# One GELU square moved a slot later, one weight split cut in two, in a fused attention and MLP kernel

## The chip, the core and the metric

The kernel runs on one core of a Trainium2 chip. The core has a matrix engine (TensorE, PE in the profile; its weight loads are PEld), a vector engine (VectorE, DVE), an engine for activation functions (ScalarE, ACT), a general engine (GpSimd, POOL) and a queue that issues transfers (SyncE, SP). Each engine works through its own queue of instructions, and they wait for one another by semaphores. The metric is the device time of one execution in microseconds (us); lower is better.

## The reference

One sequence of 2048 tokens of width 576 goes through softmax attention with 32 heads of width 18 and through an MLP with 4608 hidden units behind a layer norm; a gate mixes the two.

```python
x = A_x                                          # (1, 2048, 576)
g = sigmoid((x * gate_w).sum(-1, keepdims=True))
# a: attention, 32 heads of 18
qkv = x @ wqkv                                   # wqkv (576, 1728)
scores = einsum("bhqd,bhkd->bhqk", q, k) * 18 ** -0.5
a = (softmax(scores) @ v) @ wo                   # heads joined, wo (576, 576)
# b: MLP
h = gelu(layernorm(x) @ w1 + b1)                 # tanh form, w1 (576, 4608)
b = h @ w2 + b2                                  # w2 (4608, 576)
return g * a + (1 - g) * b
```

## The kernel before

Everything is float32. Where a product runs in the faster rounded form (float32r), an operand is split in a rounded high part and a low part, and three products are added: high by high, low by high, high by low. So every weight and activation has a copy that rounds it (on ACT) and a subtraction that leaves the rest (on DVE or POOL).

**Prologue (to 216 us).** The tokens come in four blocks of 512. For each block x is transposed, and Q, K (`qk_group`, nine groups of 128 columns) and V (`v_group`) are made and written to memory. The 1728 columns of `wqkv` come in seven pieces. `load_w` fetches a piece by three transfers (four chunks of 128 rows; the last 64 rows twice), into a buffer of which there are two. `split_w` splits it: for each run of chunks one copy on ACT (line 752) and one subtraction (line 753) on DVE, or on POOL for the fourth to the sixth piece. Each piece holds five chunks of 288 columns, 1440 elements a partition, except the narrower first and fifth. The first two pieces are split in two runs, chunks 0 to 2 and chunks 3 and 4; the others in one run. The third piece (n = 2) holds columns 416 to 703; it is split on DVE just ahead of the second `qk_group`, and the fourth group, columns 384 to 511, is the first to use it. A group multiplies chunk by chunk: the high weights by both halves of x, then the low weights by the high half, so its third matmul is the first that needs the subtraction's result. The same engines make the statistics of the layer norm there, DVE most of all.

**The loop (216 to about 2150 us).** Attention runs over 32 units (a pair of heads and half of the queries), each with 16 key chunks, in 512 steps. Beside it runs the MLP, as a stream of pieces that `fill` puts between the steps. A step has two calls of `s2`: each makes two score matmuls (line 267, one for each head of the pair, on the two halves of the array's rows) and two exponentials (line 270). After each call there is a round of the pass ahead, `s1_round`: two score matmuls (line 227), whose row maxima DVE takes (line 229); these maxima are needed for a later unit. All score tiles come from `score_bank`, which goes through five PSUM banks in turn. After every second step `pv` multiplies the probabilities of two key chunks by V (line 285).

The order is written out by hand. `run_due` closes a slot: it counts the slot, issues what was deferred to it (`defer(n, f)`: n slots later), and then background work such as weight splits. A pass over two steps has eight slots, in this order: `s2`, piece 0 of the MLP and a round, slot end; piece 1, slot end; `s2`, piece 2 and a round, slot end; piece 3, slot end; `s2`, piece 4 and a round, slot end; piece 5, slot end; `s2`, piece 6 and a round, slot end; `pv`, what is left of the maxima's transposition (line 244, copied by ACT at line 246), slot end. After this, piece 0 comes again with its `s2`.

**The hidden layer.** `h_pair` makes two tiles of 128 hidden units by 512 tokens: 27 times two matmuls (line 484). There are 72 such pairs. At a pair's end DVE adds the bias to the second tile (line 504) and ACT to the first (Identity, line 505). Then comes the tanh form of GELU for both tiles, h = 1 ahead of h = 0: ACT squares z (line 537), POOL adds a constant and multiplies by z (`first`, two instructions), ACT takes Tanh (line 535, `second`), POOL adds 1, multiplies by z, and splits the result in `hh` and `hl` (`parts`, four instructions; all of POOL's at line 180). The squares are deferred by 2 slots, `first` by 3 slots for h = 1 and by 4 for h = 0; `second` comes when a count of POOL's work says that it is through, `parts` two slots later. Pairs end mostly in piece 6, so the squares are issued behind the next `pv`.

`out_pair` multiplies `hh` and `hl` by the second weights (48 matmuls, line 572) for a group of four tiles. In its middle the two row halves of PE exchange their banks; PE waits there for a semaphore that ACT raises (line 579) when it has seen the first half's end. The groups of the hidden layer and the output products alternate: after the first pair of a group come output products of the group before, after the second pair comes the next group's first pair. In the first quarter the MLP's weights are split as they are first used (line 392 on ACT, then POOL), and written to memory, from where the later quarters load them.

Of the kernel before, what the change touches and what calls it, by code (L numbers as in the profile page):

```python
# [10 lines left out]
AF = mybir.ActivationFunctionType  # L11
# [57 lines left out]
def gated_mix_kernel(ctx: ExitStack, tc: tile.TileContext, x, wqkv, wo, w1, b1, w2, b2, gate_w, out):  # L69
    nc = tc.nc  # L70
# [42 lines left out]
    def psum(pool):  # L113
        return pool.tile([P, TB], F32, name="ps")
# [28 lines left out]
    def defer(n, fn):  # L143
        later.append((slot[0] + n, fn))
# [7 lines left out]
    def queue_end(margin, fn):  # L152
        timed.append((pool_end[0] + margin, fn))
# [23 lines left out]
    def pool_op(n, fn, *args, **kw):  # L177

        pool_end[0] = max(pool_end[0], now[0]) + n * (1.36 if fn == nc.gpsimd.tensor_scalar else 2.7)
        fn(*args, **kw)  # L180
# [155 lines left out]
    def mlp():  # L336
# [3 lines left out]
        n = len(seq)  # L340
# [3 lines left out]
        def chunk(q):  # L344

            i, m = divmod(q, G // 2)
            return i, m, seq[i][1] * G + 2 * m
# [31 lines left out]
        def rounded(dst, src):  # L379
            pool_op(src.free_size(), nc.gpsimd.tensor_scalar, dst, src, 1.0, 1.0, op0=ALU.mult, op1=ALU.mult)  # L380
# [28 lines left out]
        def ready(table, key):  # L409
            while key not in table:  # L410
                bg.pop(0)[1]()
            return table[key]
# [46 lines left out]
        def h_pair(q, last, inner=False):  # L459

            i, m, fc = chunk(q)
            tb = seq[i][0]
            while q == 0 and q not in W1:
                cut[0] = 3
                yield 0
            wt = ready(W1, q)
            del W1[q]
            ps = [psum(ps_w) for _ in range(2)]
            if q == 0:
                slots = [(w_, 0, c) for c in range(9) for w_ in (0, 1)] + [(0, 1, c) for c in range(9)]  # L470
            else:
                slots = [(w_, s_, c) for c in range(9) for w_, s_ in ((0, 0), (1, 0), (0, 1))]
            change = tb + 1 < NB and (q + 1) % (npair // NB) == 0
            loaded = 0
            left = GAPS - piece[0]
            skip.clear()
            if (last and spent[0] >= behind[0]) or left < GAPS:
                left += GAPS
            ends = {k * 27 // left for k in range(1, left)}
            for k, (w_, s_, c) in enumerate(slots):  # L480
                for h in range(2):
                    r = slice(64 * h, 64 * h + 64)
                    y = low if q < NQ0 and s_ == 1 and c < 5 else Y[s_]
                    nc.tensor.matmul(ps[h], wt[w_][r, c, :], y[r, c, :], start=(k == 0), stop=(k == 26))  # L484
                if change and (k + 1 in ends or k == 26) and (k + 1) // 3 > loaded:

                    load_y(tb + 1, 0, loaded, (k + 1) // 3)
                    load_y(tb + 1, 1, loaded, (k + 1) // 3)
                    loaded = (k + 1) // 3
                if k == 26:  # L490
                    break
                if k + 1 in ends:
                    cut[0] = 1
                yield 231
                while k == 25 and open_pairs[0]:
                    cut[0] = 3
                    yield 0
            open_pairs[0] = 1
            if inner:

                extra = wp1.tile([P, 2, 9, P], F32R, name="w4").rearrange("p a b c -> p (a b c)")
            zs = [zp.tile([P, TB], F32, name="z") for _ in range(2)]
            b = [b1t[:, fc + h:fc + h + 1] for h in range(2)]
            nc.vector.tensor_scalar(zs[1], ps[1], b[1], None, op0=ALU.add)  # L504
            nc.scalar.activation(zs[0], ps[0], AF.Identity, bias=b[0])
            for h in (1, 0):
                z = zs[h]
                w = zp.tile([P, TB], F32, name="zz", bufs=3)
                if inner:
                    hh, hl = [extra[:, (2 * h + k) * TB:(2 * h + k + 1) * TB] for k in range(2)]  # L510
                else:
                    hh = hp.tile([P, TB], F32R, name="hh")
                    hl = hp.tile([P, TB], F32R, name="hl")


                def plus(c, w, z):

                    pool_op(TB, nc.gpsimd.tensor_scalar, w, w, c, 1.0, op0=ALU.add, op1=ALU.mult)
                    pool_op(TB, nc.gpsimd.tensor_tensor, w, w, z, op=ALU.mult)

                def parts(w=w, z=z, hh=hh, hl=hl, h=h, j=2 * m + h):
                    plus(1.0, w, z)
                    rounded(hh, w)
                    pool_op(TB, nc.gpsimd.tensor_tensor, hl, w, hh.bitcast(F32), op=ALU.subtract)
                    queue_end(-1000.0, lambda: HT.update({(i, j): (hh, hl)}))
                    if h == 0:
                        open_pairs[0] = 0

                def first(w=w, z=z, parts=parts):

                    plus(GC0, w, z)
                    queue_end(200.0, lambda: second(w, parts))

                def second(w, parts):
                    nc.scalar.activation(w, w, AF.Tanh, scale=GC1)
                    defer(2, parts)
                defer(2, lambda w=w, z=z: nc.scalar.activation(w, z, AF.Square))  # L537
                defer(4 - h, first)
            cut[0] = 2
            yield 231  # L540
# [61 lines left out]
        def load_y(tb, s_, c0=0, c1=9):  # L602
            inflow[0] = slot[0]
            if s_ not in Y:
                Y[s_] = big_tile()
            for h in range(2):
                dma_r(nc.sync, Y[s_][64 * h:64 * h + 64, c0:c1, :], y_scr[tb, s_, c0:c1].rearrange("c p n -> p c n"))
# [33 lines left out]
        def pair(q, ahead, last=False, inner=False):  # L641
            prep(q + ahead)
            yield from h_pair(q, last, inner)
            i, m, _ = chunk(q)
            if m == 1 and seq[i][1] == NG - 1:
                hidden[0] = seq[i][0]
                if i == n - 1:
                    defer(1, lambda: borrow_w2(q))
# [56 lines left out]
    with ExitStack() as a:  # L705
# [41 lines left out]
        def split_w(n, eng):  # L747
            c0 = W_CUT[n] if W_CUT[n] < 2 * D else W_CUT[n] - 2 * D
            hi, lo = [w_[:, :, c0:c0 + W_CUT[n + 1] - W_CUT[n]] for w_ in (W_QK if W_CUT[n] < 2 * D else W_V)]
            raw = wraw.pop(n)  # L750
            for cs in (slice(0, 3), slice(3, 5)) if n < 2 else (slice(0, 5),):
                nc.scalar.activation(hi[:, cs], raw[:, cs], AF.Copy)
                eng.tensor_tensor(lo[:, cs], raw[:, cs], hi[:, cs].bitcast(F32), op=ALU.subtract)  # L753

# [178 lines left out]
        for c in range(5):  # L933
            x_chunk(0, c)
            if c == 2:
                split_w(0, nc.vector)
                load_w(2)
        b1r = sm.tile([NFC, P], F32, name="b1r", bufs=1)
        for tb in range(NB):
            work = [(qk_group, (tb, mt)) for mt in (range(9) if tb < 2 else (4, 0, 1, 2, 3, 5, 6, 7, 8))] + [(v_group, (tb, t, n)) for t in range(4) for n in range(2)]  # L940
            for g, (fn, args) in enumerate(work):
                if tb == 0:
                    if g in W_AT:
                        n = W_AT[g]
                        split_w(n, nc.gpsimd if 2 < n < 6 else nc.vector)
                        if n + 2 < 7:
                            load_w(n + 2)
                    if g == 10:
                        nc.sync.dma_start(b2b, bcast_rows(b2, D))
                        nc.sync.dma_start(b1r, b1.rearrange("(c p) -> c p", p=P))  # L950
# [376 lines left out]
```

## Time and profile before

| what | us |
|---|---|
| median of 3 runs | 2234.97 (2234.52 to 2236.86) |
| the profiled execution's own time | 2236.32 |
| its span, first to last instruction | 2234.4 |

Busy time in us by stretch of the span:

| stretch | length | PE | PEld | DVE | ACT | POOL |
|---|---|---|---|---|---|---|
| 0 to 20 | 20 | 15.25 | 12.33 | 7.54 | 9.47 | 10.78 |
| 20 to 60 | 40 | 38.81 | 34.50 | 30.87 | 17.04 | 14.99 |
| 60 to 216 | 156 | 155.90 | 126.83 | 108.40 | 51.33 | 42.87 |
| 216 to 690 (weights split) | 474 | 469.44 | 325.79 | 355.09 | 342.11 | 291.99 |
| 690 to 2150 | 1460 | 1457.20 | 1017.91 | 1108.40 | 977.32 | 642.56 |
| 2150 to end | 84.4 | 77.56 | 63.55 | 34.92 | 29.84 | 0.00 |

A line of the timeline gives the start in us, the time to the end of the merged instructions, the engine, the line of the kernel, the operation, the tile written and those read, the shapes, how many instructions were merged, and in brackets the engine's idle time before them with what ended it. A line of the waits gives who waited for whom: us in total, how often, the longest. In the groups by line, the numbers behind the bar are busy time, mean ns of one, and idle time before them.

### The profile page before, as it was taken

How to read it: one execution, taken by the hardware profiler on the slowest of the kernel's cores; microseconds unless marked ns; L12 is line 12 of the kernel's file. 1: busy time of each engine (PE TensorE's matmuls, PEld its weight loads, DVE VectorE, ACT ScalarE, POOL GpSimd, SP SyncE). 2: the span in 40 equal slices, each digit the busy share in tenths (PEclk: the TensorE clock that was granted, in tenths of full speed). 3: DMA queues.
4: the chain of work that ended last, by engine and by line, in shares of the span. 5: the costliest groups of instructions: out<-in, count | busy, mean ns of one | idle time of the engine just before them, and what ended most of it. 6: DMA issues, size and time to landing. Idle time of an engine off the chain costs nothing.

```text
span 2234.4 us, 51590 instructions
## 1 busy us (share of the span) xinstructions
PE 2214.2 (99%) x20528; PEld 1580.9 (71%) x20528; DVE 1645.2 (74%) x2888; ACT 1427.1 (64%) x2655; POOL 1003.2 (45%) x1001
## 2 busy tenths in 40 slices
PE   8999999999999999999999999999999999999998
PEld 7878667766667766666767767767666666776768
DVE  6675777777777777777777777777776777777734
ACT  4333677777766666666666666666666666666671
POOL 4322766666664444444445444444444444444700
PEclk9999999999999999999999999999999999999999
DMA  8867555444464533333364323232454333242264
GB/s 265 273 218 224 186 173 161 146 159 147 154 199 135 189 107 115 122 120 103 113 178 157 122 92 122 98 123 100 129 168 144 108 120 122 91 143 100 81 217 167
DMA packets 164136, 329.23 MB, mean 147 GB/s; under 512 B 56846, under 2 KB 84106, under 8 KB 153166
## 3 DMA queue, kind: packets, MB, share of 16 engines
q1 hardware_dynamic: 161798, 322.19, 44.4%
q8 instruction: 162, 2.65, 0.5%
q10 hardware_dynamic: 1968, 3.70, 0.5%
q14 instruction: 80, 0.66, 0.1%
q0 software_dynamic: 128, 0.03, 0.0%
HBM read 233.47 MB, written 96.17 MB: 148 GB/s over the span
## 4 chain that ended last, share of the span: by engine, by line
PE 92%; DVE 3%; DMA 2%; ACT 1%; issue 1%; POOL 1%; SPq 0%; ACTq 0%; DVEq 0%; POOLq 0%
PE ps L285 20%; PE ps L572 20%; PE ps L484 20%; PE ps L267 13%; PE ps L227 11%; PE ps L882 3%; PE ps L1212 2%; PE ps L903 2%; DVE m L229 1%; DMA x<-in_B_w_dram 1%; ACT zz L537 0%; POOL w L180 0%; PE ps L758 0%; DMA p<-in_A_wqkv_dram 0%; PE ps L885 0%
## 5 line engine op out<-in xcount | busy, mean ns | idle before, releaser
L229 DVE TENSOR_REDUCE m<-ps 128x1 f32<-128x512 f32 x2048 | 1312.2, 684 | 409.4 <-PE ps L227 384.8
L270 ACT ACTIVATE p<-ps 128x512 f32<-128x512 f32 x1368 | 741.0, 596 | 380.7 <-PE ps L267 376.0
L484 PE MATMUL ps<-big,w 64*128 64x512 f32 x3708 | 568.0, 393 | 1.0 <-DVE z L504 0.6
L180 POOL TENSOR_SCALAR zz<-zz 128x512 f32<-128x512 f32 x288 | 178.4, 620 | 748.8 <-ACT zz L537 734.0
L270 ACT ACTIVATE ring<-ps 128x512 f32<-128x512 f32 x680 | 369.0, 596 | 189.1 <-PE ps L267 187.0
L572 PE MATMUL ps<-w,hh 64*128 64x288 f32 x4352 | 483.9, 294 | 1.8 <-DVE x L589 0.9
L267 PE MATMUL ps<-qa,ka 56*128 56x512 f32 x2048 | 459.6, 422 | 2.9 <-ACT p L270 1.7
L572 PEld LDWEIGHTS ps<-w,hh 64*128 64x128 f32 x4352 | 423.8, 187 | 30.3 <-DVE x L589 3.2
L227 PE MATMUL ps<-ka,qa 54*128 54x512 f32 x2048 | 433.5, 398 | 0.6
L484 PEld LDWEIGHTS ps<-big,w 64*128 64x128 f32 x3708 | 368.2, 187 | 67.7 <-DVE z L504 1.1
L180 POOL TENSOR_TENSOR zz<-zz,z 128x512 f32<-128x512 f32 x288 | 371.9, 1291 | 24.0
L267 PEld LDWEIGHTS ps<-qa,ka 56*128 56x128 f32 x2048 | 213.2, 184 | 220.8 <-DVE m L229 181.0
L572 PE MATMUL ps<-w,hl 64*128 64x288 f32 x2176 | 348.3, 292 | 0.8 <-POOL hl L180 0.8
L285 PE MATMUL ps<-p,vt 128*32 128x512 f32 x2560 | 322.9, 599 | 0.0
L227 PEld LDWEIGHTS ps<-ka,qa 54*128 54x128 f32 x2048 | 218.8, 185 | 25.2 <-DVE m L229 4.5
L572 PEld LDWEIGHTS ps<-w,hl 64*128 64x128 f32 x2176 | 231.5, 185 | 1.2 <-POOL hl L180 1.1
L180 POOL TENSOR_TENSOR hl<-zz,hh 128x512 fp32r<-128x512 f32 x136 | 176.8, 1300 | 11.4
L180 POOL TENSOR_TENSOR w<-x,w 128x576 fp32r<-128x576 f32 (+1 forms) x54 | 98.8, 1845 | 168.0 <-ACT w L392 147.8
L285 PE MATMUL ps<-ring,vt 128*32 128x512 f32 x1280 | 168.7, 599 | 0.0
L285 PEld LDWEIGHTS ps<-p,vt 128*32 128x32 f32 x2560 | 67.2, 109 | 142.3 <-issue 136.1
L589 DVE SCALAR_TENSOR_TENSOR x<-ps,x 128x288 f32<-128x288 f32 x256 | 104.0, 448 | 8.6 <-PE ps L572 8.3
L882 PE MATMUL ps<-big,wqk 128*128 128x512 f32 x432 | 108.6, 400 | 0.8 <-DVE wqk L753 0.8
(124 smaller groups left out, 1491.1 us busy)
## 6 DMA issues: line engine op xcount, KB each, us to landing
w<-w_scr SPq DMA_DIRECT2D x54, 1152.0 KB
w<-w_scr SPq DMA_DIRECT2D x108, 576.0 KB
x<-in_B_w_dram SPq DMA_DIRECT2D x72, 288.0 KB
w_scr<-w SPq DMA_DIRECT2D x18, 1152.0 KB
w_scr<-w SPq DMA_DIRECT2D x36, 576.0 KB
qa<-qk_scr SPq DMA_DIRECT2D x192, 72.0 KB
ka<-qk_scr SPq DMA_DIRECT2D x84, 144.0 KB
qk_scr<-hh SPq DMA_DIRECT2D x36, 256.0 KB
```

The lines of the kernel that those rows point to most:

```text
L180: fn(*args, **kw)
L227: nc.tensor.matmul(ps, qa[r0:r0 + 54, t * P:(t + 1) * P], ka[r0:r0 + 54, kb * TB:(kb + 1) * TB], start=True, stop=True)
L229: nc.vector.tensor_reduce(M4[u][:, h, t, kb:kb + 1], ps, axis=AX.X, op=ALU.max)
L267: nc.tensor.matmul(ps[h], ka[r0:r0 + 56, kc * P:(kc + 1) * P], qa[r0:r0 + 56, qb * TB:(qb + 1) * TB], start=True, stop=True)
L270: nc.scalar.activation(RING[n % 3][:, qb, h], ps[h], AF.Exp, scale=SCALE)
L285: nc.tensor.matmul(OB[u][r:r + 32, :], v[:, k, 19 * h:19 * h + 32], RING[c % 3][:, qb, h, :], start=(k == 0), stop=(k == NT - 1))
L484: nc.tensor.matmul(ps[h], wt[w_][r, c, :], y[r, c, :], start=(k == 0), stop=(k == 26))
L572: mm = nc.tensor.matmul(ps[nn][:, :ND], h_[r, tok], w_[p_][r, cs[nn]], start=(k == 0), stop=(k == 6 * G - 1))
L589: nc.vector.scalar_tensor_tensor(dst, ps[nn][:, :ND], 0.5, b2b[:, cs[nn]] if g == 0 else dst, op0=ALU.mult, op1=ALU.add)
L882: nc.tensor.matmul(ps, w_[:, c, ms], big[:, s_, :], start=(k == 0), stop=False)
L903: nc.tensor.matmul(ps[:, :ND], big[:, s_, tok], w_[:, c, cs], start=(k == 0), stop=False)
L1212: nc.tensor.matmul(ps[:, :ND], OT[b][2][:, s_, tok], w_part(w_, c)[:, cs], start=(k == 0), stop=(k == 13))
```

## The change

The square of the second tile (h = 0) is deferred by three slots and no longer by two; that of the first tile (h = 1) stays at two. And the third weight piece is split in two runs of chunks like the first two pieces: two copies on ACT (864 and 576 elements a partition) and two subtractions on DVE, in place of one each (1440).

```diff
@@ h_pair
                 def second(w, parts):
                     nc.scalar.activation(w, w, AF.Tanh, scale=GC1)
                     defer(2, parts)
-                defer(2, lambda w=w, z=z: nc.scalar.activation(w, z, AF.Square))
+                defer(3 - h, lambda w=w, z=z: nc.scalar.activation(w, z, AF.Square))
                 defer(4 - h, first)
             cut[0] = 2
             yield 231
@@ split_w
             raw = wraw.pop(n)
-            for cs in (slice(0, 3), slice(3, 5)) if n < 2 else (slice(0, 5),):
+            for cs in (slice(0, 3), slice(3, 5)) if n < 3 else (slice(0, 5),):
                 nc.scalar.activation(hi[:, cs], raw[:, cs], AF.Copy)
                 eng.tensor_tensor(lo[:, cs], raw[:, cs], hi[:, cs].bitcast(F32), op=ALU.subtract)
```

## The prediction

> **What bounds the kernel now.** I read the page first, then the list of what PE waited for, then ACT and PE in order of time at the places where the moved square stands, and last the first 45 us.
>
> ```profile
> span 2234.4 us, 51590 instructions
> PE 2214.2 (99%) x20528; PEld 1580.9 (71%) x20528; DVE 1645.2 (74%) x2888; ACT 1427.1 (64%) x2655; POOL 1003.2 (45%) x1001
> PE 92%; DVE 3%; DMA 2%; ACT 1%; issue 1%; POOL 1%; SPq 0%; ACTq 0%; DVEq 0%; POOLq 0%
> ```
>
> PE is busy for 99% of the span and makes 92% of the chain that ended last. So ACT, at 64%, matters only where PE must wait for one of its results. PE's own waits are short:
>
> ```profile
> PE ps L267 <- ACT p L270: 1.7, 8, 0.3
> PE ps L572 <- POOL hl L180: 0.8, 1, 0.8
> PE ps L882 <- DVE wqk L753: 0.8, 1, 0.8
> ```
>
> In the loop these rows hold a few microseconds in all, for ACT's exponentials 1.7 us in 8 waits; in the prologue 0.8 us behind the very line that the second edit splits. These figures are too small, though, since a PE row counts as busy until a modelled end. The first place below shows it: a matmul slips by 0.57 us, and the idle column says 0.18.
>
> How ACT makes PE wait: scores go through five PSUM banks in turn, an exponential pair takes two and a maximum round takes two. The second score matmul of a pair therefore writes the bank that the first exponential of the pair before has to have read. That exponential's end is the deadline that counts.
>
> **Edit 1, the second square, where a transpose stands ahead.** At a pair's end ACT runs Identity (L505), both squares (L537), then two exponential pairs, then Tanh (L535). Now the second square goes behind the first exponential pair. Nothing is added: 72 squares change place in ACT's queue, no DMA is moved, and neither SP's queue nor any other is passed. In 8 of the 72 pair ends the copy of the row maxima (L246) stands ahead of the squares, for the first time at 460 us and for the last at 1813 us. One of them:
>
> ```profile
> 460.19 0.27 ACT L246 ACTIVATE mr<-ps 32x128 fp32r<-32x128 f32 x1 [1.52 <-PE ps L244]
> 1813.31 0.27 ACT L246 ACTIVATE mr<-ps 32x128 fp32r<-32x128 f32 x1 [1.05 <-PE ps L244]
> ...
> 1012.26 1.13 ACT L537 ACTIVATE zz<-z 128x512 f32<-128x512 f32 x2
> 1013.30 2.00 ACT L270 ACTIVATE p<-ps 128x512 f32<-128x512 f32 x4
> 1013.35 0.40 PE L267 MATMUL ps<-qa,ka 56*128 56x512 f32 x1
> 1013.92 0.49 PE L267 MATMUL ps<-qa,ka 56*128 56x512 f32 x1 [0.18 <-ACT p L270]
> 1015.12 0.57 PE L267 MATMUL ps<-qa,ka 56*128 56x512 f32 x2
> ```
>
> The squares take the exponentials' time: four of them run without a gap, 0.48 us apart and 0.57 long. The first ends at 13.30 + 0.57 = 13.87 (I leave off the 1000), and PE's second matmul, which should have come with its partner at 13.35, starts at 13.92: 0.05 us for the semaphore, 0.57 us lost. After the change the first exponential starts one square earlier, 0.52 us, at 12.78; the matmul needs 12.78 + 0.57 + 0.05 = 13.40, so only 0.05 is lost. The square then costs the second pair: it starts at 12.78 + 0.48 + 0.48 + 0.52 = 14.26, as now, while PE comes 0.52 earlier. The next pair's second matmul, at 15.29 now (15.12 + 0.57 less a length of 0.40), would come at 14.77 and has to wait until 14.26 + 0.57 + 0.05 = 14.88: 0.11 lost. Net gain 0.41 us. At 460 us a Tanh and a weight copy right behind give it all back. I count 7 x 0.35 = 2.5 us gained, 0.35 because the halves of PE run out of step there.
>
> The Trainium skill (Trainium Kernel Development and Optimization, section "Performance Expectations") says that matmul busy time is a bad measure of the distance to the roofline, because matmuls are pipelined. The trace agrees: the row shows 0.18 us idle where 0.57 were lost. By busy time alone edit 1 could win 1.7 us at most; by the starts it is more.
>
> **Edit 1 elsewhere.** Where no transpose stands ahead, ACT has time to spare before the first exponential pair, and none or little behind it:
>
> ```profile
> 1050.31 1.15 ACT L537 ACTIVATE zz<-z 128x512 f32<-128x512 f32 x2
> 1051.90 1.09 ACT L270 ACTIVATE p<-ps 128x512 f32<-128x512 f32 x2 [0.45 <-PE ps L267]
> 1053.07 1.09 ACT L270 ACTIVATE ring<-ps 128x512 f32<-128x512 f32 x2
> 1054.04 0.63 ACT L535 ACTIVATE zz<-zz 128x512 f32<-128x512 f32 x1
> 1054.56 1.09 ACT L270 ACTIVATE ring<-ps 128x512 f32<-128x512 f32 x2
> 1054.05 0.40 PE L267 MATMUL ps<-qa,ka 56*128 56x512 f32 x2
> 1055.44 0.41 PE L267 MATMUL ps<-qa,ka 56*128 56x512 f32 x2
> 1051.02 0.62 POOL L180 TENSOR_SCALAR zz<-zz 128x512 f32<-128x512 f32 x1 [25.89 <-ACT zz L537]
> 1051.72 1.29 POOL L180 TENSOR_TENSOR zz<-zz,z 128x512 f32<-128x512 f32 x1
> ```
>
> Here the square now runs in a hole (0.45 us idle behind it) and is put into a dense stretch. It starts 0.12 us before the pair's end (Tanh to its neighbours shows this overlap: 54.04 against 53.07 + 1.09), at 52.87, and holds ACT 0.52 us (two squares in 1.15, one 0.63). The second pair moves from 53.07 to 53.39, Tanh and the third pair by the same 0.32. First deadline: 53.39 + 0.60 + 0.05 = 54.04 against 54.05, just kept. Second: 54.88 + 0.60 + 0.05 = 55.53 against 55.46 (the second of the pair, 0.02 behind its partner): 0.07 us lost. ACT's next idle time ends it. I count 21 such places from 690 us on: 1.5 us lost.
>
> Where weights are still being split, a weight copy (L392) follows that Tanh, and PE is already late:
>
> ```profile
> 515.67 1.09 ACT L270 ACTIVATE p<-ps 128x512 f32<-128x512 f32 x2
> 516.64 0.63 ACT L535 ACTIVATE zz<-zz 128x512 f32<-128x512 f32 x1
> 517.17 0.68 ACT L392 ACTIVATE w<-x 128x576 fp32r<-128x576 f32 x1
> 517.74 1.08 ACT L270 ACTIVATE p<-ps 128x512 f32<-128x512 f32 x2
> 518.04 0.84 PE L267 MATMUL ps<-qa,ka 56*128 56x512 f32 x2
> ```
>
> PE's pair takes 0.84 us instead of 0.40, its second matmul at 517.74 + 0.59 + 0.05 = 518.38. Every 0.32 us more is lost in full. Four places (351, 513, 567, 621 us): 1.3 us.
>
> Where products with the second weight follow (30 places), the dense stretch has a gap:
>
> ```profile
> 1066.07 1.09 ACT L270 ACTIVATE ring<-ps 128x512 f32<-128x512 f32 x2 [0.22 <-PE ps L267]
> 1067.34 1.09 ACT L270 ACTIVATE p<-ps 128x512 f32<-128x512 f32 x2 [0.18 <-PE ps L267]
> 1068.17 0.41 PE L267 MATMUL ps<-qa,ka 56*128 56x512 f32 x2
> L579 ACTq EVENT_SEMAPHORE  x1: 17/17/17, 1068.1 to 1068.1; - x1
> ```
>
> The square runs from 67.04, the second pair from 67.56 instead of 67.34, its first end with the semaphore at 68.21 against 68.18: 0.03 us each, 0.9 in all. The few other places I set at -0.2 us together.
>
> POOL waits for these squares, but it starts with the first one, which doesn't move, and needs 0.70 + 1.29 us (51.02 to 53.01) before it asks for the second; that now ends at 53.50 instead of 51.46, so POOL's work on it starts about 0.5 us late. The cover is POOL's idle time, 25.89 us at this place; without it, 0.5 us at each pair, 36 us. What waits behind the square on ACT is counted above; its own inputs are old.
>
> Edit 1: -2.5 + 1.5 + 1.3 + 0.9 - 0.2 = +1.0 us. Its bounds: all eight gains in full and no loss, 8 x 0.57 = -4.6 us; and 0.32 us at all of the 64 other places, +20 us. I stay with the sum, since it goes place by place.
>
> **Edit 2, the third weight piece.** Five chunks of 288 columns go through one copy on ACT and one subtraction on DVE; PE's fourth group waits for the whole.
>
> ```profile
> 17.61 1.41 ACT L752 ACTIVATE wqk<-p 128x1440 fp32r<-128x1440 f32 x1 [4.00 <-DMA p<-in_A_wqkv_dram]
> 10.53 1.49 ACT L752 ACTIVATE wqk<-p 128x864 fp32r<-128x864 f32 x2
> 19.05 1.66 DVE L753 TENSOR_TENSOR wqk<-p,wqk 128x1440 fp32r<-128x1440 f32 x1 [4.72 <-ACT wqk L752]
> 11.48 1.73 DVE L753 TENSOR_TENSOR wqk<-p,wqk 128x864 fp32r<-128x864 f32 x2
> 19.34 0.63 PE L882 MATMUL ps<-big,wqk 128*128 128x512 f32 x2
> 20.76 2.59 PE L882 MATMUL ps<-big,wqk 128*128 128x512 f32 x10 [0.80 <-DVE wqk L753]
> PEld ps L903 <- DVE wv L753: 0.4, 1, 0.4
> ```
>
> The second piece has the same size and is already cut: its two copies take 1.49 us, its two subtractions 1.73. So the split costs 0.08 us on ACT and 0.07 on DVE. By elements the first part is 3/5: 0.9 us of copy from 17.61 to 18.51, then 1.04 us of subtraction to about 19.6, the rest to 18.54 + 1.73 = 20.27 instead of 20.71. PE's third matmul of that group wants it at 19.34 + 2 x 0.235 = 19.81 (0.63 for two, less a length of 0.40, is the spacing) and started at 20.76: 0.95 us gained there. DVE is dense behind it, so its work comes 0.44 us earlier, and PE next waits for DVE at the last weight piece (L903, 0.4 us). There only DVE's 0.44 is kept. The first part no longer needs the two last transfers and may start before 17.61. I take -0.5; the bounds are +0.1 (extra instructions, nothing kept) and -1.0.
>
> **Sum.** +1.0 - 0.5 = +0.5 us on the profiled execution's own 2236.32 us (span 2234.4 and 1.9 around it). That execution is 1.35 us above the median of 2234.97. Carried to the median: 2235.5 us, which is no change; 0.2% (4.5 us) is about what a measurement of this kernel can tell from none.
>
> **The rivals.** *The bank swap waits for ACT (slower).* In the middle of an output product PE waits for a semaphore that ACT raises (L579), queued behind the second exponential pair. At 1068.1 it comes 0.2 us after that pair's last exponential was taken (67.34 + 0.49 = 67.83) and before its end at 68.43, so nothing shows that it waits for the end. Were it to wait for the end, each of the 39 pair ends with products behind would lose about 0.3 us: +12 us, 2247. It decides once the pair is later than the slack to PE's next half. *ACT's order was what delayed PE (faster).* If the exponentials behind the square keep their deadlines by other slack, no loss stands against the gains: -4.6 - 1.0, 2229.4 on the median. For it: both deadlines are missed by under 0.1 us. Against it: PE at 518 us is late already. *The loss is everywhere as with the weight copies (slower):* 0.32 us at all 25 pair ends of the first kind, +8.0 - 2.5 + 0.9 - 0.7: 2240.7. Against it: only 4 have a weight copy.
>
> **How the numbers follow.** Forecast 0.66; the swap 0.10 and the loss everywhere 0.08, both slower; the faster one 0.16. These give faster 0.16, within 0.2% 0.66, slower 0.18. The range goes from the faster rival to beyond the smaller slow one and leaves the swap out: 2229 to 2243.
>
> **What would show it.** ACT reads Identity, square, two exponentials, square at the pair ends. Near 1012 us the pair of score matmuls starts together; near 1050 us the second exponential pair starts 0.3 us later after the first; near 518 us PE's pair grows from 0.84 to about 1.15 us. Near 20 us PE's 0.80 us is gone, and the 0.4 us at L903 has grown. PE's waits for L579 stay near none. It is wrong if the semaphore rows of L579 move to the exponentials' ends, or if POOL's late half reaches PE (waits for hl above 0.8 us).

## The result, and the profile after

The changed kernel takes 2244.85 us (median of 5 runs, 2244.2 to 2247.33) against 2235.09 before (5 runs, 2234.52 to 2236.86): 1.0043 times the time of before, 95% interval 1.0032 to 1.0054. It is slower by some 10 us; I had forecast no change, and 2229 to 2243 as the range. The profiled execution took 2245.5 us, with a span of 2243.6 against 2234.4, so 9.2 us are to be found.

The page of the changed kernel, span, busy times and the chain by engine:

```profile
span 2243.6 us, 51653 instructions
PE 2223.8 (99%) x20528; PEld 1597.8 (71%) x20528; DVE 1649.8 (74%) x2889; ACT 1416.6 (63%) x2656; POOL 1003.0 (45%) x1001
PE 90%; DVE 3%; DMA 2%; ACT 2%; issue 1%; POOL 1%; SPq 0%; ACTq 0%; POOLq 0%; DVEq 0%
```

PE is "busy" for 9.6 us more with the same 20528 matmuls. So the loss sits inside what the page counts as busy, and the busy share alone can't show it. What PE's matmuls (PE) and its weight loads (PEld) waited for, after:

```profile
PE ps L267 <- ACT p L270: 1.8, 6, 0.4
PEld ps L267 <- ACT p L270: 8.5, 28, 0.8
PEld ps L267 <- ACT ring L270: 5.6, 19, 1.0
PE ps L572 <- POOL hl L180: 0.6, 1, 0.6
```

The same list before, for the weight loads:

```profile
PEld ps L267 <- ACT p L270: 7.3, 17, 0.7
PEld ps L267 <- ACT ring L270: 3.2, 7, 1.0
```

The matmuls wait for ACT hardly more than before, but their weight loads do 47 times in place of 24. The product with V is a good ruler for a stretch, as it needs both halves of PE. Two successive ones stand around the pair end that the prediction read near 1050 us. Before:

```profile
1049.52 1.07 PE L285 MATMUL ps<-ring,vt 128*32 128x512 f32 x8
1056.49 1.07 PE L285 MATMUL ps<-p,vt 128*32 128x512 f32 x8
```

and after:

```profile
1051.99 1.07 PE L285 MATMUL ps<-ring,vt 128*32 128x512 f32 x8
1059.21 1.07 PE L285 MATMUL ps<-p,vt 128*32 128x512 f32 x8
```

6.97 us became 7.22: 0.25 us lost at this one pair end, where I had worked out 0.07. Measured in this way at all 72 pair ends (PE's start 8.5 us behind the squares less its start 0.5 us ahead of them, after against before):

| pair ends | count | lost, us | predicted, us |
|---|---|---|---|
| hidden pair follows, no transpose ahead | 30 | 6.1 (0.23 each at most places) | 1.5 + 1.3 |
| output products follow, no transpose ahead | 34 | 5.3 (0.17 each at most places) | 0.9 |
| transpose ahead of the squares | 8 | -2.0 | -2.5 |
| prologue, to the loop's start | | -0.4 | -0.5 |

(The prediction's other places, -0.2, fall into the first two rows.) The four add up to 9.0 of the 9.2 us. The rest of the loop loses another 0.6 us (eight places, shown by the experiment with a late POOL, lose 0.9 there), and the stretch behind 2150 us is 0.4 us shorter.

### The profile page after: what moved, and what is told of

Same layout as the page of the kernel before. It is cut to its first block, busy times and chain, and to the rows that moved or that the text cites. A ratio compares the mean times of both kernels' runs of the same rounds, so it can differ in the third digit from the quotient of the medians.

```text
span 2243.6 us, 51653 instructions
## 1 busy us (share of the span) xinstructions
PE 2223.8 (99%) x20528; PEld 1597.8 (71%) x20528; DVE 1649.8 (74%) x2889; ACT 1416.6 (63%) x2656; POOL 1003.0 (45%) x1001
## 4 chain that ended last, share of the span: by engine, by line
PE 90%; DVE 3%; DMA 2%; ACT 2%; issue 1%; POOL 1%; SPq 0%; ACTq 0%; POOLq 0%; DVEq 0%
PE ps L285 20%; PE ps L572 19%; PE ps L484 19%; PE ps L267 13%; PE ps L227 11%; PE ps L882 3%; PE ps L1212 2%; PE ps L903 1%; DVE m L229 1%; DMA p<-in_A_wqkv_dram 1%; ACT p L270 0%; POOL w L180 0%; POOL zz L180 0%; DMA x<-in_B_w_dram 0%; PE ps L758 0%
## 5 line engine op out<-in xcount | busy, mean ns | idle before, releaser
L484 PE MATMUL ps<-big,w 64*128 64x512 f32 x3708 | 579.5, 393 | 1.0 <-DVE z L504 0.6
L572 PE MATMUL ps<-w,hh 64*128 64x288 f32 x4352 | 501.1, 293 | 1.8 <-DVE x L589 0.9
L267 PE MATMUL ps<-qa,ka 56*128 56x512 f32 x2048 | 480.5, 427 | 3.4 <-ACT p L270 1.8
L572 PEld LDWEIGHTS ps<-w,hh 64*128 64x128 f32 x4352 | 442.1, 186 | 27.2 <-DVE x L589 3.2
L227 PE MATMUL ps<-ka,qa 54*128 54x512 f32 x2048 | 454.0, 398 | 0.6
L484 PEld LDWEIGHTS ps<-big,w 64*128 64x128 f32 x3708 | 381.5, 187 | 60.9 <-DVE z L504 1.1
L267 PEld LDWEIGHTS ps<-qa,ka 56*128 56x128 f32 x2048 | 232.8, 184 | 227.0 <-DVE m L229 181.0
L572 PE MATMUL ps<-w,hl 64*128 64x288 f32 x2176 | 368.8, 292 | 0.6 <-POOL hl L180 0.6
L572 PEld LDWEIGHTS ps<-w,hl 64*128 64x128 f32 x2176 | 253.1, 185 | 1.0 <-POOL hl L180 0.8
L227 PEld LDWEIGHTS ps<-ka,qa 54*128 54x128 f32 x2048 | 233.7, 185 | 22.9 <-DVE m L229 5.3
```

Of the source, the lines that this page charges most:

```text
L227: nc.tensor.matmul(ps, qa[r0:r0 + 54, t * P:(t + 1) * P], ka[r0:r0 + 54, kb * TB:(kb + 1) * TB], start=True, stop=True)
L267: nc.tensor.matmul(ps[h], ka[r0:r0 + 56, kc * P:(kc + 1) * P], qa[r0:r0 + 56, qb * TB:(qb + 1) * TB], start=True, stop=True)
L572: mm = nc.tensor.matmul(ps[nn][:, :ND], h_[r, tok], w_[p_][r, cs[nn]], start=(k == 0), stop=(k == 6 * G - 1))
```

## What the trace shows at one pair end

ACT near 1050 us of the old count, changed kernel:

```profile
1052.78 0.63 ACT L537 ACTIVATE zz<-z 128x512 f32<-128x512 f32 x1
1054.44 1.09 ACT L270 ACTIVATE p<-ps 128x512 f32<-128x512 f32 x2 [1.03 <-PE ps L267]
1055.41 0.63 ACT L537 ACTIVATE zz<-z 128x512 f32<-128x512 f32 x1
1055.93 1.09 ACT L270 ACTIVATE ring<-ps 128x512 f32<-128x512 f32 x2
1056.88 0.65 ACT L535 ACTIVATE zz<-zz 128x512 f32<-128x512 f32 x1
1057.40 1.11 ACT L270 ACTIVATE ring<-ps 128x512 f32<-128x512 f32 x2
```

The order is the predicted one. The hole ahead of the first exponential pair has grown from 0.45 to 1.03 us, and behind it there is none: the second pair starts 1.49 us behind the first in place of 1.17, 0.32 later, as predicted. PE and its weight loads there, after:

```profile
1053.85 0.50 PE L267 MATMUL ps<-qa,ka 56*128 56x512 f32 x2
1055.11 0.47 PE L267 MATMUL ps<-qa,ka 56*128 56x512 f32 x2
1056.30 0.46 PEld L267 LDWEIGHTS ps<-qa,ka 56*128 56x128 f32 x2
1056.53 0.56 PE L267 MATMUL ps<-qa,ka 56*128 56x512 f32 x2
1057.93 0.64 PE L267 MATMUL ps<-qa,ka 56*128 56x512 f32 x2
```

and the second of them before, for the matmuls at 1054.05 that the prediction shows:

```profile
1053.83 0.19 PEld L267 LDWEIGHTS ps<-qa,ka 56*128 56x128 f32 x2
```

Before, both weight loads of the pair start together at 53.83, 0.22 us ahead of the matmuls. After, the first starts at 56.30 and the second, 0.18 long, not before 56.30 + 0.46 - 0.18 = 56.58. That is the end of the first exponential, 55.93 + 0.60 = 56.53, and 0.05 for the semaphore. So it is the weight load that waits for the bank.

How late may it be? The pair before this one answers that, since one of its two weight loads is late in the kernel before as well:

```profile
1052.55 0.18 PEld L267 LDWEIGHTS ps<-qa,ka 56*128 56x128 f32 x1
1052.64 0.41 PE L267 MATMUL ps<-qa,ka 56*128 56x512 f32 x2
1052.64 0.21 PEld L484 LDWEIGHTS ps<-big,w 64*128 64x128 f32 x2
```

Its partner started at 52.41, so this load is 0.14 us behind, and 0.09 us ahead of the matmul. The next weight loads (L484) are 0.19 long; the first starts at 52.64 together with the matmul, the second at 52.64 + 0.21 - 0.19 = 52.66, 0.11 us behind the late load. So only 0.02 us is lost. The three pairs in question, after:

```profile
1055.09 0.18 PEld L267 LDWEIGHTS ps<-qa,ka 56*128 56x128 f32 x1
1055.12 0.27 PEld L484 LDWEIGHTS ps<-big,w 64*128 64x128 f32 x2
1056.58 0.18 PEld L267 LDWEIGHTS ps<-qa,ka 56*128 56x128 f32 x1
1056.58 0.29 PEld L484 LDWEIGHTS ps<-big,w 64*128 64x128 f32 x2
1058.07 0.18 PEld L267 LDWEIGHTS ps<-qa,ka 56*128 56x128 f32 x1 [0.19 <-ACT ring L270]
1058.18 0.19 PEld L484 LDWEIGHTS ps<-big,w 64*128 64x128 f32 x2
```

Each late load comes 0.05 us behind the end of an exponential and now hardly ahead of its own matmul (at 55.12, 56.59 and 58.08). The matmul's row still starts on time, and so hides the loss, but the next weight load of that half again follows 0.11 us behind the late one (at 55.20, 56.68 and 58.18). The half is set back by 0.07, 0.10 and 0.09 us at the three pairs, less the 0.02 of before: 0.24 us together, about one matmul, and the product with V, for which both halves must be through, turns it into lost time. The matmul pairs show the growing lag: they take 0.47, 0.56 and then 0.64 us in place of 0.41. So the deadline is not the start of the matmul but some 0.11 us ahead of it. Over the whole trace a pair's second weight load starts less than 0.1 us ahead of its matmul 314 times before and 407 times after, and in 402 of the 407 the next weight load follows it by 0.10 to 0.12 us.

## The experiments

**Each edit alone.** The first run has the change's first edit, the second its second, on the kernel before:

```diff
-                defer(2, lambda w=w, z=z: nc.scalar.activation(w, z, AF.Square))
+                defer(3 - h, lambda w=w, z=z: nc.scalar.activation(w, z, AF.Square))
```

> Edit 1 alone: the second square a slot later, the third weight piece in one run as before. Theory A (ACT's queue: the square stands in ACT's dense stretch, the exponentials behind it come too late for PE's weight loads): all of the loss and none of the prologue's gain of 0.4 us, so 2245.3 us against 2235.1 before. Theory B (POOL: its work on the second tile starts 0.5 us later and reaches PE late): also 2245.3. Theory C (the split weight piece costs the time further on): 2235, as before.

```diff
-            for cs in (slice(0, 3), slice(3, 5)) if n < 2 else (slice(0, 5),):
+            for cs in (slice(0, 3), slice(3, 5)) if n < 3 else (slice(0, 5),):
```

> Edit 2 alone: the third weight piece in two runs, both squares where they were. A and B: 0.4 us faster than before, 2234.7, with PE's 0.8 us wait for the third piece gone. C: 2245.

The square alone: 2247.23 against 2236.09 us, ratio 1.0047 (1.0032 to 1.0062); a second time 1.0046 (1.0032 to 1.0060). The split alone: 2235.82, ratio 0.9997 (0.9988 to 1.0007). Theory C is out, the square makes the whole loss. By the trace the split does what it was to do (PE in the fourth group, changed kernel; before, the row broke off behind two matmuls):

```profile
19.47 2.73 PE L882 MATMUL ps<-big,wqk 128*128 128x512 f32 x11
17.04 1.50 ACT L752 ACTIVATE wqk<-p 128x864 fp32r<-128x864 f32 x2 [3.31 <-DMA p<-in_A_wqkv_dram]
18.00 1.73 DVE L753 TENSOR_TENSOR wqk<-p,wqk 128x864 fp32r<-128x864 f32 x2 [3.54 <-ACT wqk L752]
```

PE runs through, and the copy starts at 17.04 in place of 17.61, as the first run no longer needs the two last transfers. The loop starts 0.4 us earlier in the changed kernel and 0.9 us earlier with the split alone; in the traces without the split it starts between 0.3 us earlier and 0.6 us later than before, so the size of the gain is not settled, and on the whole time it is less than a comparison can show.

**ACT or POOL?** The next two pull the two theories apart. One lets ACT do a second square at the new place, and POOL wait for nothing new:

```diff
                 defer(2, lambda w=w, z=z: nc.scalar.activation(w, z, AF.Square))
+                if h == 0:
+                    defer(3, lambda hh=hh, z=z: nc.scalar.activation(hh, z, AF.Square))
```

> Both squares as before, and a second copy of the h = 0 square, written into a tile that POOL overwrites later, at the slot to which the change moves the square. POOL waits for nothing new. A: the loss of 0.2 us at 64 pair ends stays, and at the 8 with a transpose ahead there is now a loss of 0.5 us in place of a gain: 13 + 4, 2252 us. B: 2235, since POOL starts as before.

The other makes POOL late and leaves ACT's order as it was:

```diff
-                def first(w=w, z=z, parts=parts):
+                def first(w=w, z=z, parts=parts, h=h, hh=hh):
 
+                    if h == 0:
+                        nc.gpsimd.tensor_scalar(hh, z, 1.0, 1.0, op0=ALU.mult, op1=ALU.mult)
                     plus(GC0, w, z)
```

> Both squares as before, and one more POOL instruction (a rounding copy of 512 elements, 0.7 us with its gap) ahead of POOL's work on the second tile, so that all its work from there is 0.7 us later, more than the 0.5 us of the change. A: 2235 within 1 us. B: at least the loss of the change, 2245 to 2249.

The extra square: 2247.74 us, ratio 1.0050 (1.0035 to 1.0065). The loss stays with POOL as before, so ACT's queue is the cause of most of it; it is smaller than expected, 0.11 us at a pair end with output products behind and 0.18 with a hidden pair, for 0.17 and 0.24 with the moved square, and 1.6 us over the 8 with a transpose ahead, where 4 were expected. POOL late: 2240.89 us, ratio 1.0024 (1.0014 to 1.0033), where theory A had said 1 us at most. Neither theory had this. At the pair ends it loses next to nothing (1.0 us over all 72), but 4.0 us at 8 of the 32 transpositions of the row maxima (others than the 8 with squares behind them). DVE there, with POOL late:

```profile
1073.05 0.83 DVE L238 CAST nmh<-nm 128x16 fp32r<-128x16 f32 x1
```

and before:

```profile
1071.22 0.25 DVE L238 CAST nmh<-nm 128x16 fp32r<-128x16 f32 x1
```

and POOL, with POOL late:

```profile
1072.56 1.29 POOL L180 TENSOR_TENSOR zz<-zz,z 128x512 f32<-128x512 f32 x1
```

DVE's small copy takes 0.83 us in place of 0.25 and ends with POOL's instruction, at 1073.9. In all twelve traces of this case every such copy that took over 0.18 us, 127 of them, ends 0.02 to 0.05 us behind the end of a POOL instruction; where no POOL instruction runs beside it, it takes 0.17 to 0.18. That the one holds up the other is read from this, and no run tried it by itself.

The changed kernel has the same at the same 8 places, on a smaller scale. After:

```profile
1073.94 0.57 DVE L238 CAST nmh<-nm 128x16 fp32r<-128x16 f32 x1
PEld ps L244 <- DVE nm L240: 9.0, 10, 1.2
```

and the wait of PE's weight loads for the end of this DVE work before:

```profile
PEld ps L244 <- DVE nm L240: 6.3, 7, 1.2
```

At seven of the 8 places the copy takes 0.57 to 0.88 us, in place of 0.22 to 0.47. From the product with V ahead of the copy to the next one, the 8 together lose 0.9 us in the changed kernel and with the square alone, 4.0 with POOL late, and nothing with the extra square (0.2 gained), where POOL is on time. So about 1 us of the change's loss does come by POOL, at these places and not at the pair ends.

**More and less of it.** Both squares at the later slot double the suspected cost; the square cut in two, with one half at the old place, halves it.

```diff
-                defer(2, lambda w=w, z=z: nc.scalar.activation(w, z, AF.Square))
+                defer(3, lambda w=w, z=z: nc.scalar.activation(w, z, AF.Square))
```

> Both squares a slot later, so that two of them stand between the first and the second exponential pair; weight pieces as before. The suspected cost doubled. If what counts is ACT's time in that stretch, nothing covers the second square: 0.5 us more at each of 64 pair ends on top of the change's 0.2, less the gains at the 8 others: 2275 to 2280 us. If only the order or the wait that the move brings cost the time, about as the change, 2246.

```diff
-                defer(2, lambda w=w, z=z: nc.scalar.activation(w, z, AF.Square))
+                defer(2, lambda w=w, z=z, n=TB if h else TB // 2: nc.scalar.activation(w[:, :n], z[:, :n], AF.Square))
+                if h == 0:
+                    defer(3, lambda w=w, z=z: nc.scalar.activation(w[:, TB // 2:], z[:, TB // 2:], AF.Square))
```

> The second square cut in two instructions of 256 columns, the first where it was, the other a slot later. The suspected cost halved: some 0.3 us of ACT between the exponential pairs in place of 0.52, of which the stretch's idle time covers most. ACT's time counts: under 0.1 us at the 64 pair ends, 0.2 us gained at the 8: 2235 to 2239. If the order alone counts: as the change, 2246.

Both late: 2316.0 us, ratio 1.0356 (1.0341 to 1.0372), far above the 2280 expected. ACT there:

```profile
1098.65 1.09 ACT L270 ACTIVATE p<-ps 128x512 f32<-128x512 f32 x2
1100.35 0.63 ACT L535 ACTIVATE zz<-zz 128x512 f32<-128x512 f32 x1 [0.62 <-POOL zz L180]
1100.89 2.04 ACT L270 ACTIVATE p<-ps 128x512 f32<-128x512 f32 x4
```

With the first square moved too, POOL starts so late that Tanh has to wait for it, and Tanh stands ahead of two exponential pairs: POOL's lateness comes back to PE through ACT's queue. The wait of Tanh for POOL sums to 37.7 us here, and to 0.8 before and in the changed kernel. The halves: 2236.47 us, ratio 1.0001 (0.9992 to 1.0010), with the exponential pairs 1.28 us apart in place of 1.17 and nothing lost:

```profile
1051.38 1.09 ACT L270 ACTIVATE p<-ps 128x512 f32<-128x512 f32 x2 [0.66 <-PE ps L267]
1052.35 0.42 ACT L539 ACTIVATE zz<-z 128x256 f32<-128x256 f32 x1
1052.66 1.09 ACT L270 ACTIVATE ring<-ps 128x512 f32<-128x512 f32 x2
```

Its second pair's first exponential gives its bank back at 52.66 + 0.60 + 0.05 = 53.31, and the matmuls come at 53.53, so it is 0.22 us ahead, more than the 0.11 that are needed. The exponential pair, 0.11 us later than before, costs nothing here; 0.32 us later it does.

**The second wait.** The first exponential behind the lone square waits for two semaphores, of which one is ACT's own, and starts 0.59 us behind its matmul (1054.44 less 1053.85) in place of 0.53. The second wait is an instruction of its own, and the exponentials' line has 61 more of these, after and before:

```profile
L270 ACTq EVENT_SEMAPHORE  x613: 17/17/17, 220.2 to 2187.6; - x154
L270 ACTq EVENT_SEMAPHORE  x552: 17/17/17, 220.6 to 2177.9; - x184
```

A square of one column at the old place takes that wait away:

```diff
                 defer(3 - h, lambda w=w, z=z: nc.scalar.activation(w, z, AF.Square))
+                if h == 0:
+                    defer(2, lambda w=w, z=z: nc.scalar.activation(w[:, :1], z[:, :1], AF.Square))
```

> Edit 1 alone, and a square of one column of the h = 0 tile at the old place, right behind the first square. In the changed kernel the first exponential behind the lone square carries a second wait, on ACT's own semaphore, and starts 0.59 us after its matmul in place of 0.53. The tiny square takes that wait. If these 0.06 us are part of the loss, as the comparison of the change with the extra square says (0.17 and 0.24 us lost at a pair end against 0.11 and 0.18), about 4 us of the 11 come back and 1 goes at the 8 pair ends with a transpose ahead: ratio to before 1.003 to 1.004. If the wait costs nothing, or only the square's own time counts: as edit 1 alone, 1.0047.

> Edit 1 alone once more, on the same chip as the run with the tiny square, for comparison: 1.0047.

2243.26 us, ratio 1.0033 (1.0021 to 1.0046), beside 1.0046 for edit 1 alone on the same chip; the intervals overlap, but the trace has the gain where it was expected. The separate waits are 552 again, and the exponentials start 1054.47 - 1053.93 = 0.54 us behind their matmuls:

```profile
1053.40 0.19 ACT L539 ACTIVATE zz<-z 128x1 f32<-128x1 f32 x1
1054.47 1.09 ACT L270 ACTIVATE p<-ps 128x512 f32<-128x512 f32 x2 [0.88 <-PE ps L267]
1053.93 0.51 PE L267 MATMUL ps<-qa,ka 56*128 56x512 f32 x2
```

and the usual loss at a pair end falls to 0.11 and 0.17 us, that of the extra square. From 690 us on, the 48 pair ends without a transpose lose 6.6 us in place of 9.4: 0.06 us at each.

**The other way.** If the square belongs ahead of the dense stretch, then both may go ahead of the transpose too:

```diff
-                defer(2, lambda w=w, z=z: nc.scalar.activation(w, z, AF.Square))
+                defer(1, lambda w=w, z=z: nc.scalar.activation(w, z, AF.Square))
```

> Both squares a slot earlier, right behind the Identity and ahead of the copy of the row maxima; weight pieces as before. No square stands then ahead of an exponential that is due. ACT's time counts: nothing changes at the 64 pair ends, and the 0.5 to 0.6 us lost at each of the 8 others is gone: 4 to 5 us faster than before, 2231. If a square's distance to POOL's work mattered instead, no change.

> Both squares a slot earlier, and the third weight piece in two runs as in the change. The sum of two gains in different stretches: 4 to 5 us and 0.4 to 0.9 us, 2230.

Both squares early: 2231.4 us against 2236.27, ratio 0.9979 (0.9969 to 0.9988), faster than both kernels. With the split as well: 2232.03 us, 0.9980 (0.9971 to 0.9989), no better, where 2230 was expected. By its trace it enters the loop 0.6 us earlier than with the squares alone, but the stretch behind 2150 us is 2.5 us longer than before; with the split alone that stretch was 2.1 us shorter, so it varies by more than the split gives. The same pair end as the prediction's 1012 us, squares early:

```profile
1009.75 1.15 ACT L537 ACTIVATE zz<-z 128x512 f32<-128x512 f32 x2 [0.31 <-DVE z L504]
1010.80 0.25 ACT L246 ACTIVATE mr<-ps 32x128 fp32r<-32x128 f32 x1
1010.96 1.05 ACT L270 ACTIVATE p<-ps 128x512 f32<-128x512 f32 x2
1011.76 0.39 PE L267 MATMUL ps<-qa,ka 56*128 56x512 f32 x2
```

The exponentials follow the copy of the maxima at once, and the next pair of matmuls starts together. These 8 pair ends gain 4.4 us of the 4.9, and the 64 others stay as they were (0.2 us over all).

## Why the prediction was wrong

- **The order, the hole and the shift** were right: the square left a hole (0.45 became 1.03 us) and made the second exponential pair 0.32 us later.
- **The deadline failed**, in the sentences "First deadline: 53.39 + 0.60 + 0.05 = 54.04 against 54.05, just kept" and "0.07 us lost", and in the same way at 1068 us with "0.03 us each". I held the end of an exponential against the start of the matmul that writes its bank. What waits is that matmul's weight load, and it has to start some 0.11 us ahead of the matmul. With this in my own working the first deadline is 54.05 - 0.11 = 53.94, missed by 0.10 us, and the second, with PE 0.10 later by then, is 55.46 + 0.10 - 0.11 = 55.45, missed by 0.08; the trace has 0.10 and 0.09. At 1068 us 0.03 becomes 0.14, where the extra square lost 0.11. So a place that I called just kept was already missed, and most of the 64 losses were sized too small: 11.4 us in all where I had 3.5 (1.5 + 1.3 + 0.9 - 0.2).
- **A term was missing**: the exponential behind the lone square starts 0.06 us later for a second wait. By the run with the tiny square this is 2.8 us at the 48 pair ends from 690 us on, and 0.06 at all 64 would be 3.8; the rest of the 7.9 us that were missing, some 4 us, is left for the deadline.
- **Where a matmul already waited**, the sum held: at the four places with a weight copy 0.34 to 0.39 us were lost at each, predicted 0.32; at the transposes 2.0 us gained, predicted 2.5: six of the 8 gain 0.31 to 0.40 us, and two nothing, the one at 460 us as foreseen and one at 1625. There the stall in the trace of before was itself the measure, whatever caused it.
- **POOL** stays covered at the pair ends, as said: Tanh's wait for POOL is unchanged, and PE's for hl is 0.6 us. What I left out is that a later POOL meets DVE's small copies at 8 transpositions, about 1 us.
- **The split** gave 0.4 us up to the loop, predicted 0.5. One sign failed: PE's wait at L903 did not grow, it is 0.3 us in place of 0.4.
- **The rivals**: the one with the loss everywhere came nearest, with 0.32 us at 25 places for the true 0.17 to 0.24 at most of 64; its reason, a weight copy, was not the one at work. The bank swap was wrong: weight loads wait for L579 5 times and 1.0 us in all, as before. The Trainium skill's rule on busy time (Trainium Kernel Development and Optimization, section "Performance Expectations") held better than I used it: PE is "busy" for 9.6 us more and does nothing more.

The deadline 0.11 us ahead of the matmul was read from the traces, and it fits the runs with half, whole and extra square; no run moved the weight load itself, so why the next load follows 0.11 us behind a late one stays open.

## What to carry to other kernels

When a result frees a bank for a matmul, count back to the matmul's weight load and not to the matmul's start, and look at the waits of the weight loads when a full matrix engine gets slower. On an engine with an in-order queue, put work that nobody waits for into the hole ahead of the dense stretch, as early as its inputs allow; a few tenths of a microsecond between two deadlines come back at every repetition. And where a trace shows a stall of the same kind already, size by that stall rather than by a margin that seems just enough.

## What was not expected of the hardware

- A matmul's row starts on time even if its weight load came too late; the loss shows at the next weight load, 0.11 us behind the late one. Three such misses of 0.07 to 0.10 us on one half of PE became 0.23 to 0.25 us by the time both halves were needed.
- The small DVE instructions between two score rounds seem to depend on what POOL does at that moment: a copy of 16 elements a partition takes 0.17 us by itself, and up to 1.1 us when it ends with a POOL instruction that overlaps it. A POOL that was 0.7 us later cost 4.8 us, most of it at such places.
- A second semaphore wait ahead of an ACT instruction cost 0.06 us even though what it waited for was long done.
